# A fused convolution and linear-attention kernel: the first x group loaded and transposed in two pairs, another order of the first loads, six warm-up matmuls for nine, and a new written-out schedule

## The chip, the core and the metric

The kernel runs on one NeuronCore of a Trainium2 chip. The core has five instruction queues that run side by side and meet only at semaphores: PE (TensorE, matmuls and transposes into PSUM), DVE (VectorE), ACT (ScalarE), POOL (GpSimd) and SP (SyncE, which here issues every DMA). The metric is the device time of one execution in microseconds (us), lower is better; a time is the median of several runs.

## The reference

Two independent heads over a sequence of 2048 rows and 576 channels, put side by side in the output:

```python
def _A_ref(q, k, v, shift_k, ssm_k, ssm_D):
    k_pad = jnp.pad(k, ((0, 0), (ks - 1, 0), (0, 0)))
    for t in range(ks):                                   # ks = 4
        k_shift = k_shift + k_pad[:, t:t + S, :] * shift_k[:, ks - 1 - t]
    kv = k_shift * v
    y = irfft(rfft(kv, 2 * S) * rfft(ssm_k, 2 * S))[:S]   # long causal convolution
    y = y + kv * ssm_D
    return q * y

def _B_ref(x, wqkv, wo):                                  # 32 heads of 18 channels
    q, k, v = split(x @ wqkv)
    phi = lambda t: jnp.where(t > 0, t + 1, jnp.exp(t)) + 1e-6
    pq, pk = phi(q), phi(k)
    kv = jnp.einsum("bhsd,bhse->bhde", pk, v)
    z = jnp.einsum("bhsd->bhd", pk)
    num = jnp.einsum("bhqd,bhde->bhqe", pq, kv)
    den = jnp.einsum("bhqd,bhd->bhq", pq, z)[..., None] + 1e-6
    return (num / den) @ wo
```

All inputs are bf16.

## The kernel before

Both heads are written as one list of about 830 operations (`P.op`), each with the buffers it reads and writes. No scheduler runs: the text `PLAN` names the operations in the order in which they are issued, each with a letter for its engine (P for PE, A for ACT, D for DVE, G for POOL, S for SP), and `PLACES` gives the address of every buffer, PSUM banks included. Each engine therefore works through its own list strictly in the order written; an operation that may run on either of two engines ("AD", "DG") runs on the one whose letter the plan has. A buffer that reuses an address waits for the last user of it.

Head B. x is taken in four groups of 512 rows. `xt_load(g)` loads group g into `x_sb` (rows 4p to 4p+3 on partition p) and makes its transpose `xT`, which the projections need. For groups 1 to 3 (`XD`) a transposing DMA makes `xT`. For group 0, PE makes it: 16 transposes of 128x128 from `x_sb0` (L330) and four from `x40` (L328), where `x40` is a copy of channels 512 to 575 beside a block of ones; each of three PSUM tiles is then copied to `xT0` on DVE or ACT (L230 or L228). `kproj(r)` multiplies 128 rows by the key weights `wk` (ten matmuls, L606), ACT takes the exponential (`ek`, L611), and DVE makes the key feature in `pk` (L614). `qproj` does the same for queries (L627, L630, L633). `b_G(t)` (L656) contracts all of `x_sb` with all of `pk`: its first matmul needs the last of the 16 key features. After it come the small products (kv, z, den, M, msf), the normalisation of the queries through DRAM (`rden`, `rb`, `pqn`), and the output projection `b_out` (L796), whose rows leave through `ob`.

Head A is a Fourier transform in two matmul steps. The filter is transposed on PE (L419, copied to `hT`), step one is `s1` (L450, copied to `Ch` or `Cu` by ACT or DVE), then a 32x32 transpose on DVE (L489, `ct`), then step two (L498, copied to `sph` or `spu`). The key convolution is done on DVE in six pieces: two tap products (L389), two additions and the product with v (L235; some of these on POOL). Spectra are multiplied (`p1`, `p2`, L235), transformed back by `inv` (L534, copied to `V`) and `inv2` (L559), multiplied by q and stored.

The kernel starts with nine matmuls on a constant tile (`fill`, L827), whose result nobody reads; they need only a DVE memset of `cft` (L823). The first loads on SP are, in this order: x group 0, the constant tile `idw` (the identity and two small matrices), the shift weights `srow`, the tail of `wk` (channels 512 to 575, 72 KB) and then its main part (channels 0 to 511, 576 KB), two pieces of the filter (`hs`), the tail of `wq`, `Drow`, the main part of `wq`, the tables `Gsb`.

Of the kernel before, what the change touches and what calls it, by code (L numbers as in the profile page):

```python
# [9 lines left out]
BF = mybir.dt.bfloat16  # L10
# [4 lines left out]
D = 576  # L15
# [167 lines left out]
def kernel(  # L183
# [39 lines left out]
    def load(name, b, fn, nb, row, wr=None, rd=(), after=(), engs="S"):  # L223
        return P.op(engs, fn, rd=rd, wr=[b] if wr is None else wr, name=name, after=after, nb=nb, row=row)
# [79 lines left out]

    def xt_load(g):
        load("x", x_sb[g], lambda e: dma(e, x_sb[g].t[:].rearrange("p a d -> p (a d)"),
# [13 lines left out]
        for t0, tn in ((0, 2), (2, 2), (4, 1)):  # L320
            ps = psb(1, "xps")

            def tr(e, t0=t0, tn=tn, ps=ps):
                o = ps.t.rearrange("p b c -> p (b c)").bitcast(BF)
                for j in range(tn):
                    for i in range(4):
                        if t0 == 4:
                            nc.tensor.transpose(out=o[:, 128 * i:128 * i + 128], in_=x4[g].t[:, i, :], identity=ident())  # L328
                        else:
                            nc.tensor.transpose(out=o[:, 512 * j + 128 * i:512 * j + 128 * i + 128],  # L330
                                                in_=x_sb[g].t[:, i, 128 * (t0 + j):128 * (t0 + j) + 128], identity=ident())

            def ev(e, t0=t0, tn=tn, ps=ps):
                o = ps.t.rearrange("p b c -> p (b c)").bitcast(BF)
                copy(e, b.t[0:KT[t0], t0:t0 + tn, :].rearrange("p t n -> p (t n)"), o[0:KT[t0], 0:512 * tn])
            P.op("P", tr, rd=[(x4[g], "m"), (x4[g], "o"), idw] if t0 == 4 else [(x_sb[g], "m"), idw], wr=[ps], name="xtr", mm=[(128, 128, 128)] * (4 * tn), st="xtr%d" % g)
            P.op("DA", ev, rd=[ps], wr=[(b, t0)], name="xev", n=512 * tn, x2=1, st="xtr%d" % g)
# [259 lines left out]
    def kproj(r):  # L597
# [12 lines left out]
        P.op("P", mm, rd=[xT, wk], wr=[ps], name="k", mm=[(288, 128, 128)] * 10, st=st)  # L610
# [214 lines left out]
    def fmm(e):  # L825
        for j in range(9):
            nc.tensor.matmul(fps.t[:, 0, :], lhsT=cft.t[:, 0:128], rhs=cft.t[:], start=True, stop=True)  # L827
    P.op("P", fmm, rd=[cft], wr=[fps], name="fill", mm=[(512, 128, 128)] * 9)
# [24 lines left out]
G3 G4 S26 G6 G10 G5 G12 G1 D832 G14 G53 G8 S16 S18 P833 A27 P28 D29 P30 S50 P32 D31 S49 S361 S367 G2 A33 S52 P100  # L853
G9 G0 S21 P94 P97 P362 D23 A101 P368 A15 D102 A95 G224 D363 A98 S51 S19 G7 D99 A369 S20 D366 P91 A92 G11 P371 S419
A370 D96 A372 D93 G374 P364 A373 S474 P142 D365 A143 P376 D377 G375 P384 A385 P378 D379 D144 P145 A146 P386 D147
P382 D387 P380 S55 P148 G13 S37 P422 A383 A381 S36 P388 A149 D423 S24 P390 P420 P477 S468 A389 S47 D150 P439 G38
D421 P437 A391 A478 G424 P435 D440 P427 D436 S56 S42 A438 G48 S25 P433 D410 A428 S54 D392 P425 A426 P475 P431 A434
D476 P429 A430 P157 P471 P417 A432 P413 P399 D401 A472 A400 P395 P397 A398 S41 A414 A396 P469 D441 P166 D470 P444
S46 A158 S57 P408 P163 P393 P448 S39 D450 D409 A418 D159 P406 A167 A164 A407 D168 P151 A449 S44 A152 P442 A445 D165
P446 S226 P402 G43 G473 A443 G479 A447 D459 P139 P460 P160 A403 D153 A394 D71 S34 P415 P451 D70 A161 A140 P457 D162  # L860
A461 A416 D141 A452 P169 A458 P178 P453 P466 A454 P462 A463 P455 D72 P464 A456 D60 A465 P193 A467 P187 A170 P411
P404 S17 D61 A405 A412 A179 P109 P196 A194 A188 D180 P175 S225 D189 A197 G73 D171 S670 P184 S570 D195 A110 S669
D111 S628 A40 A185 G45 A176 D62 P112 P127 A113 D114 P172 D177 D186 P121 D198 P103 A128 G74 D129 A173 A122 D63 P181
D174 D123 P115 G35 P190 A104 G64 A182 D183 D105 A116 S569 D117 D81 P490 P130 A491 D80 A131 P492 P124 S549 A493 A125
P154 D132 P133 P118 S58 D126 S228 A155 A191 A134 A119 D82 P136 A137 D135 D156 S227 D120 D138 P106 A107 P482 P488
A483 D192 D108 G83 D84 P480 A481 P494 P219 D66 D65 A495 S59 S649 D75 A489 P486 S648 A220 P484 A487 P222 D76 P199
A223 A221 P232 D234 D233 D77 D78 A485 P204 A205 A206 P235 G79 A200 D236 D237 P239 D240 P207 P604 D238 A208 D241
P612 A613 S627 A201 S243 P214 D67 D68 A605 P614 P616 S242 D215 P602 S548 S256 D69 P217 D86 D85 D87 A615 A603 D88
D89 A617 P606 P610 P608 S255 A216 S244 A218 A611 P212 P533 S267 A609 P525 A607 A526 P535 A534 A536 S250 P209 G268
A210 A211 S254 P523 A524 P531 P202 S246 D245 A532 D514 P527 D496 P683 A213 A203 A528 G251 P695 A696 P229 D660 A684  # L870
P693 S252 D231 A694 P687 D230 P685 G247 A686 P277 P269 D688 D278 P689 A270 P273 P275 A274 P271 A276 D690 P515 P661
A272 A662 P681 A682 S263 G264 P691 S261 D253 S248 P279 D505 S259 G249 P503 A516 D692 P663 P497 P501 P667 A504 P508
A664 D280 A502 D509 P529 P298 D498 P311 P537 G262 P303 D639 G260 D299 A530 P306 A668 A538 D618 D539 A312 A307 P288
P665 A304 S257 P625 S22 P646 A289 P619 P621 A622 G258 P506 D620 A507 A626 P499 S265 P313 D581 S590 P308 A314 P286
D647 D560 A666 A309 A287 S90 S315 P283 S591 A284 P296 A297 S300 P623 P584 P510 G266 D500 S290 P586 S707 P540 P640
P321 A624 A541 D587 P323 A585 P318 D511 G671 A641 A322 P561 A319 A562 P563 A564 P519 P565 D739 P546 P642 P333 D566
A324 A547 D643 P336 A520 P326 P281 A334 A327 A282 P517 D337 D672 P512 A513 S727 P644 P544 P521 S706 P542 D518 A522
A545 A543 A645 P746 D697 P328 P353 P356 A357 D747 P346 P702 P567 A329 D354 A703 P704 P588 D718 S325 A589 A347 P700
P740 A741 P316 P293 A294 A701 A568 S749 A317 S285 S330 P291 P348 P358 A292 P338 A359 A705 S728 A349 S310 S320 A339
P673 G630 D629 P633 D650 P351 D651 P582 P744 D550 A674 P721 P742 D551 A634 P725 P331 A745 A583 P675 P301 S748 A743  # L880
P637 D726 S350 A676 A332 A302 P677 P719 A638 D572 P698 A352 P723 P679 P554 A678 A699 D750 P658 S360 D571 A724 P652
A720 P631 D592 D555 P656 A722 P552 A632 P556 P635 D593 P654 D751 A659 P558 A653 D553 A557 A657 P598 D636 A655 A680
S335 P600 P596 A597 A601 S340 A599 D709 P594 P573 P758 P798 A799 P784 D574 D708 A595 P575 S295 P579 P756 A785 P792
D576 D757 P577 A580 P796 S305 A559 P790 A578 P786 D730 D729 A787 P802 A791 D788 S355 A803 A797 P712 P768 P714 P710
A713 P762 D793 P774 A715 A769 A711 P766 D763 P780 G800 A775 S789 A759 P804 P760 D767 D770 S801 P731 S771 A805 P735
A736 D794 D761 D781 S795 P772 D764 A773 P778 S765 P737 D806 D776 P754 D755 A732 A779 P716 P752 P733 A717 A738 A753
P341 D782 P343 D734 D342 S807 A344 S777 S783 S345 P810 P808 D809 P826 P828 A811 P816 A829 D812 S813 P822 A823 D827
A817 P820 D830 S831 D821 D824 S825 D818 P814 D815 S819
"""
PLACES = """  # L890
# [47 lines left out]
```

## Time and profile before

| | us |
|---|---|
| median of 3 runs | 161.12 (161.06 to 161.38) |
| the profiled execution | 161.13 |
| its span, first to last instruction | 159.3 |
| around the span | 1.83 |

The profile is of one execution. Its page gives busy time by engine; the windows give the same for any stretch of time; the timeline lists the instructions in order; the chain of waits is followed back from the last instruction, and names at each step what released it. Matmuls overlap, and the page models their ends, so that PE counts as busy while it works through a queue slowly: a high PE share alone doesn't say that PE sets the pace. Where the records of two neighbouring instructions of one engine overlap by some hundredths of a microsecond, the distance of their starts is what they cost.

### The profile page before, as it was taken

What the parts mean: (1) busy time and instruction counts of PE and PEld (TensorE: products, weight loads), DVE (VectorE), ACT (ScalarE), POOL (GpSimd) and SP (SyncE); (2) the same over time, 40 slices, a digit from 0 to 9 for tenths busy, and PEclk for the clock granted to TensorE, in tenths of its full rate; (3) what the DMA queues carried; (4) which work ended last, traced back from release to release, by engine and by line L of the source; (5) the groups of instructions that cost most, each with busy time, mean ns of one, the idle gap of its engine ahead of it and who ended that gap; (6) DMA issues with size and microseconds to landing.
All of it is one profiled execution on the core that took longest, in us unless ns stands there. A gap on an engine that the chain in (4) does not pass through costs nothing.

```text
span 159.3 us, 4148 instructions
## 1 busy us (share of the span) xinstructions
PE 150.7 (95%) x1663; PEld 119.0 (75%) x1663; DVE 142.9 (90%) x173; ACT 126.5 (79%) x235; POOL 54.7 (34%) x48
## 2 busy tenths in 40 slices
PE   6899999999999999999999998999999999999980
PEld 2588888544568888788788887676677979999970
DVE  1318989999989999999999999999999999998981
ACT  3247899999997577784169799898999999889960
POOL 8802311200065940700340049899929000004000
PEclk9999999999999999999999999999999999999997
DMA  5999988999999204998014336864987735001875
GB/s 178 304 372 383 140 159 257 351 149 258 406 341 399 81 4 134 368 264 296 10 50 150 112 117 218 261 207 123 375 285 285 260 111 191 0 4 49 220 211 154
DMA packets 25629, 32.80 MB, mean 206 GB/s; under 512 B 15754, under 2 KB 20875, under 8 KB 24842
## 3 DMA queue, kind: packets, MB, share of 16 engines
q1 hardware_dynamic: 25610, 32.54, 67.8%
q8 instruction: 13, 0.21, 0.5%
q14 instruction: 6, 0.05, 0.1%
HBM read 20.86 MB, written 4.99 MB: 162 GB/s over the span
## 4 chain that ended last, share of the span: by engine, by line
PE 60%; DVE 26%; ACT 5%; DMA 3%; issue 2%; SPq 1%; DVEq 0%
PE ps_all L656 12%; PE ps_all L796 11%; PE ps_all L534 10%; PE ps_all L450 8%; DVE pqT L633 6%; DVE ct L489 5%; PE ps_all L559 5%; DVE pk L614 5%; DVE m L389 4%; PE ps_all L627 3%; PE ps_all L498 3%; PE ps_all L606 3%; DMA wk<-in_B_wqkv_dram 3%; DVE m L235 2%; PE ps_all L419 2%
## 5 line engine op out<-in xcount | busy, mean ns | idle before, releaser
L627 PE MATMUL ps_all<-xT,wq 128*126 128x512 bf16 (+1 forms) x100 | 24.5, 382 | 0.0
L796 PE MATMUL ps_all<-M,pqT 126*128 126x288 bf16 (+1 forms) x160 | 21.9, 287 | 0.3 <-ACT spu L228 0.3
L606 PE MATMUL ps_all<-wk,xT 128*128 128x288 bf16 x160 | 21.1, 286 | 0.6 <-DMA wk<-in_B_wqkv_dram 0.6
L389 DVE TENSOR_TENSOR m<-kh,Wj 128x3072 bf16<-128x3072 bf16 x12 | 20.5, 1754 | 0.0
L796 PEld LDWEIGHTS <-pqT 126*128 126x128 bf16 (+1 forms) x160 | 16.8, 110 | 4.6 <-issue 2.7
L606 PEld LDWEIGHTS <-xT 128*128 128x128 bf16 x160 | 17.4, 110 | 3.6 <-issue 1.0
L450 PEld LDWEIGHTS <-Gsb 128*128 128x128 bf16 x192 | 16.2, 98 | 4.0 <-issue 2.2
L228 ACT ACTIVATE Cu<-ps_all 128x768 bf16<-128x768 f32 x21 | 16.6, 862 | 1.7 <-PE ps_all L450 1.0
L627 PEld LDWEIGHTS <-wq 128*126 128x126 bf16 (+1 forms) x100 | 12.3, 131 | 7.3 <-issue 1.5
L534 PE MATMUL ps_all<-Esb,sph 128*128 128x128 bf16 x144 | 17.2, 219 | 0.0
L534 PE MATMUL ps_all<-Esb,X 128*128 128x128 bf16 x144 | 17.1, 219 | 0.0
L656 PE MATMUL ps_all<-pk,x_sb 128*128 128x289 bf16 (+1 forms) x128 | 17.1, 287 | 0.0
L235 POOL TENSOR_TENSOR pqT<-pqT,rb 126x1024 bf16<-126x1024 bf16 (+1 forms) x8 | 16.8, 2132 | 0.8 <-DVE pqT L235 0.6
L611 ACT ACTIVATE ek<-ps_all,neg 128x576 bf16<-128x576 f32 x16 | 11.9, 742 | 6.5 <-PE ps_all L606 5.6
L228 ACT ACTIVATE spu<-ps_all 128x512 bf16<-128x512 f32 x29 | 16.2, 620 | 0.7 <-DVE ct L489 0.7
L228 ACT ACTIVATE V<-ps_all 128x512 bf16<-128x512 f32 x28 | 15.8, 635 | 0.8 <-PE ps_all L534 0.4
L228 ACT ACTIVATE Ch<-ps_all 128x768 bf16<-128x768 f32 x19 | 15.3, 862 | 1.4 <-POOL v L235 1.0
L228 ACT ACTIVATE sph<-ps_all 128x512 bf16<-128x512 f32 x30 | 16.1, 628 | 0.4 <-PE ps_all L498 0.3
L630 ACT ACTIVATE eq<-ps_all,neg 126x512 bf16<-126x512 f32 (+1 forms) x20 | 13.2, 701 | 1.8 <-PE ps_all L627 1.8
L656 PEld LDWEIGHTS <-x_sb 128*128 128x128 bf16 x128 | 12.3, 98 | 3.2 <-issue 0.2
L235 DVE TENSOR_TENSOR m<-m 128x3072 bf16<-128x3072 bf16 (+1 forms) x10 | 14.4, 1442 | 0.1
L534 PEld LDWEIGHTS <-sph 128*128 128x128 bf16 x144 | 14.1, 98 | 0.4 <-issue 0.4
(94 smaller groups left out, 294.3 us busy)
## 6 DMA issues: line engine op xcount, KB each, us to landing
X<-sph SPq DMA_DIRECT2D x18, 256.0 KB
x_sb<-in_B_x_dram SPq DMA_DIRECT2D x4, 576.0 KB
v<-in_A_v_dram SPq DMA_DIRECT2D x2, 1152.0 KB
q<-in_A_q_dram SPq DMA_DIRECT2D x1, 2304.0 KB
out_dram<-ob SPq DMA_DIRECT2D x16, 144.0 KB
out_dram<-q SPq DMA_DIRECT2D x12, 192.0 KB
rb<-r_scr SPq DMA_DIRECT2D x8, 252.0 KB
kh<-in_A_k_dram SPq DMA_DIRECT2D x1, 1584.0 KB
```

The source lines that it names most:

```text
L228: nc.scalar.activation(out=o, in_=i, func=ACTF.Copy)
L235: return (nc.vector if e == "DVE" else nc.gpsimd).tensor_tensor(out=o, in0=a, in1=b, op=op)
L389: return nc.vector.tensor_tensor(out=m.t[:, i:i + 2], in0=i0, in1=i1, op=ALU.mult)
L450: nc.tensor.matmul(ps.t[:, bank, lo - 384 * bank:hi - 384 * bank], lhsT=Gsb.t[:, b, ri, :], rhs=src[:, lo - CC * j:hi - CC * j], start=Tru ...
L534: nc.tensor.matmul(ps.t[:, 0, 128 * c:128 * c + 128], lhsT=src.t[:, 4 * hh + c, :], rhs=Esb.t[:, 32 + wi, :], start=(wi == 0), stop=(wi == 1))
L606: nc.tensor.matmul(ps.t[:, hh, 0:HALF], lhsT=cols(xT.t[0:KT[t], t, :], r), rhs=wk.t[0:KT[t], t, HALF * hh:HALF * hh + HALF], start=(t == 0 ...
L611: P.op("A", lambda e: nc.scalar.activation(out=eb.t[:], in_=ps.t[:, :, 0:HALF], func=ACTF.Exp, bias=neg1.t[:]), rd=[ps, neg1], wr=[eb], na ...
L627: nc.tensor.matmul(ps.t[0:hn, 0, :], lhsT=wq.t[0:KT[t], t, h0:h0 + hn], rhs=xT.t[0:KT[t], t, :], start=(t == 0), stop=(t == 4))
L630: P.op("A", lambda e: nc.scalar.activation(out=eb.t[0:hn], in_=ps.t[0:hn, 0, :], func=ACTF.Exp, bias=neg1.t[0:hn, :]), rd=[ps, neg1], wr=[eb],
L633: P.op("D", lambda e: nc.vector.scalar_tensor_tensor(out=pqT[g // 2].t[0:hn, c, 512 * (g % 2):512 * (g % 2) + 512], in0=eb.t[0:hn], scalar ...
L656: nc.tensor.matmul(ps.t[0:m, 0, 0:n], lhsT=x4[r // 4].t[:, r % 4, :] if t == 4 else x_sb[r // 4].t[:, r % 4, 128 * t:128 * t + 128], rhs=p ...
L796: nc.tensor.matmul(ps.t[:, 0, 0:HALF], lhsT=cols(pqT[r // 8].t[0:kn, c, 512 * (r // 4 % 2):512 * (r // 4 % 2) + 512], r), rhs=M.t[0:kn, c, ...
```

## The change

- Group 0 goes through a new function, `x_pairs`. Its load is two DMAs of two rows per partition each, its copy to `x40` is two copies, and its transposes fill four PSUM tiles: for each pair one of eight transposes (channels 0 to 511) and one of two (from `x40`), each with its own copy to `xT0`.
- `kproj` of group 0 waits only for the pair that holds its rows, not for all of `xT0`.
- Six matmuls on the constant tile in place of nine.
- `PLAN` and `PLACES` are new throughout. Operations keep what they compute, but order, engines and addresses differ. (Operation numbers are four higher than before from about operation 35 on, since x_pairs adds four.)

The first loads on SP become: the second pair of x, `idw`, the first pair, the main part and then the tail of `wk`, two `hs`, half of `Gsb`, `Drow`, a third `hs`, the other half of `Gsb`, `srow`, then `wq` around a fourth `hs`. On DVE, `x_pairs` gives two copies to `x40` and four to `xT0`, one after the other (first pair's large copy, its small one, the second pair's small one, its large one). On PE the order behind the transposes is: key products of rows 0, 2 and 1, four filter tiles, and then steps one of the filter's transform; the fourth key product and all query products of group 0 come behind these, where before they stood ahead of them or between them.

```diff
+    def x_pairs(g):
+        b = SB("xT%d" % g, [128, 5, 512])
+        xTg.append(b)
+        for p in range(2):
+            load("xp", x_sb[g], lambda e, p=p: dma(e, x_sb[g].t[:, 2 * p:2 * p + 2].rearrange("p a d -> p (a d)"),
+                                                   ap(x, 512 * g * D + 2 * p * D, [[4 * D, 128], [1, 2 * D]])),
+                 294912, 2304, wr=[(x_sb[g], p)], engs=EARLY)
+            P.op("GDA", lambda e, p=p: copy(e, x4[g].t[:, 2 * p:2 * p + 2, 64:128], x_sb[g].t[:, 2 * p:2 * p + 2, 512:576]),
+                 rd=[(x_sb[g], p), (x4[g], "o")], wr=[(x4[g], ("m", p))], name="x4c", n=128, st="xtr%d" % g)
+        for p in range(2):
+            for t0, tn in ((0, 4), (4, 1)):
+                ps = psb(1, "xps")
+
+                def tr(e, t0=t0, tn=tn, ps=ps, p=p):
+                    o = ps.t.rearrange("p b c -> p (b c)").bitcast(BF)
+                    for j in range(tn):
+                        for i in range(2):
+                            nc.tensor.transpose(out=o[:, 256 * j + 128 * i:256 * j + 128 * i + 128],
+                                                in_=x4[g].t[:, 2 * p + i, :] if t0 == 4 else x_sb[g].t[:, 2 * p + i, 128 * j:128 * j + 128],
+                                                identity=ident())
+
+                def ev(e, t0=t0, tn=tn, ps=ps, p=p):
+                    o = ps.t.rearrange("p b c -> p (b c)").bitcast(BF)
+                    copy(e, b.t[:, t0:t0 + tn, 256 * p:256 * p + 256], o[:, 0:256 * tn].rearrange("p (t n) -> p t n", t=tn))
+                P.op("P", tr, rd=[(x4[g], ("m", p)), (x4[g], "o"), idw] if t0 == 4 else [(x_sb[g], p), idw], wr=[ps], name="xtr",
+                     mm=[(128, 128, 128)] * (2 * tn), st="xtr%d" % g)
+                P.op("DA", ev, rd=[ps], wr=[(b, (p, t0))], name="xev", n=256 * tn, x2=1, st="xtr%d" % g)
+
     def xt_load(g):
+        if g not in XD:
+            return x_pairs(g)
...
-        for t0, tn in ((0, 2), (2, 2), (4, 1)):
-            ps = psb(1, "xps")
...
-            P.op("P", tr, rd=[(x4[g], "m"), (x4[g], "o"), idw] if t0 == 4 else [(x_sb[g], "m"), idw], wr=[ps], name="xtr", mm=[(128, 128, 128)] * (4 * tn), st="xtr%d" % g)
-            P.op("DA", ev, rd=[ps], wr=[(b, t0)], name="xev", n=512 * tn, x2=1, st="xtr%d" % g)
...
-        P.op("P", mm, rd=[xT, wk], wr=[ps], name="k", mm=[(288, 128, 128)] * 10, st=st)
+        P.op("P", mm, rd=[wk] + ([xT] if r // 4 in XD else [(xT, (r % 4 // 2, t0)) for t0 in (0, 4)]), wr=[ps], name="k", mm=[(288, 128, 128)] * 10, st=st)
...
     def fmm(e):
-        for j in range(9):
+        for j in range(6):
...
-    P.op("P", fmm, rd=[cft], wr=[fps], name="fill", mm=[(512, 128, 128)] * 9)
+    P.op("P", fmm, rd=[cft], wr=[fps], name="fill", mm=[(512, 128, 128)] * 6)
...
 PLAN = """
-G3 G4 S26 G6 G10 G5 G12 G1 D832 G14 G53 G8 S16 S18 P833 A27 P28 D29 P30 S50 P32 D31 S49 S361 S367 G2 A33 S52 P100
...
+D836 G0 G57 G13 S28 G7 G11 G6 P837 S16 G5 S26 G1 A15 S53 S54 G9 P34 P30 G2 D29 G3 D27 P36 G14 D31 P32 D33 G8 P95
...
```

More of the change, by code (lines that the diff above doesn't have):

```diff
@@ L319, in xt_load @@
             return
-        for t0, tn in ((0, 2), (2, 2), (4, 1)):
-            ps = psb(1, "xps")
[L323 to L335, printed above, removed]
-            P.op("P", tr, rd=[(x4[g], "m"), (x4[g], "o"), idw] if t0 == 4 else [(x_sb[g], "m"), idw], wr=[ps], name="xtr", mm=[(128, 128, 128)] * (4 * tn), st="xtr%d" % g)
-            P.op("DA", ev, rd=[ps], wr=[(b, t0)], name="xev", n=512 * tn, x2=1, st="xtr%d" % g)
     def wload(which, key):
@@ L858 @@
[L858 to L872, printed above, removed]
@@ new lines @@
+P167 A114 A201 A192 D75 A168 G47 D199 G67 D115 P185 G483 D160 P122 A123 D193 P173 A174 D166 A49 D169 D76 A186 P107
+A108 G68 P179 D124 D187 S43 D202 D175 P137 D109 A180 A138 P134 S231 D77 D181 S38 G44 P119 S229 D139 G78 A135 D136
+P176 A120 S230 A177 P490 D121 P188 P494 A491 D178 A189 S652 A39 P496 A497 P110 P182 A495 A111 D84 D85 P488 A489
+S553 A183 D112 D86 S17 S62 P125 P140 A126 P128 S632 A141 D127 D87 D142 G88 D190 P131 A129 D130 A132 D184 P116 D133
+A117 P484 A485 S631 P194 S594 P535 P498 D118 P492 A493 A499 A195 S653 P223 D70 A224 P226 D69 P486 A487 A227 D196
@@ L889 @@
+P577 D584 P562 A578 P824 D825 S823 P285 S829 D286 S289 A563 P770 P772 A773 P766 A767 D771 D774 P764 P776 P778 A765
+D768 S775 S769 A779 A777 D780 P784 S781 P782 A785 A783 D786 S787
 """
 PLACES = """
[16 rows of a table removed]
[16 rows of a table added]
 """
```

48 lines of the change are left out of this document (28 added, 20 removed), and 32 rows, old and new, of the table PLACES.

## The prediction

> **What bounds the kernel now.** I read the page first, then the windows, the chain of waits and the timeline. By busy time PE is in front:
>
> ```profile
> PE 150.7 (95%) x1663; PEld 119.0 (75%) x1663; DVE 142.9 (90%) x173; ACT 126.5 (79%) x235; POOL 54.7 (34%) x48
> ```
>
> The reader is to see that two engines are nearly full, and that neither is named by its share alone, since stretched matmuls count as busy. The windows, cut where the first key feature starts on DVE, where DVE begins its transposes, where the last key feature ends, and where the last matmul ends, tell more (columns: window; its length, then busy us and count of PE, PEld, DVE, ACT, POOL; clock; DMA share; GB/s):
>
> ```profile
> 0.00:10.24 10.24, 8.13 (x48) 5.09 (x49) 1.95 (x5) 3.07 (x5) 6.55 (x20) 1.00 0.80 268
> 10.24:24.56 14.32, 14.31 (x150) 12.15 (x149) 11.89 (x18) 11.94 (x19) 2.47 (x5) 1.00 1.14 238
> 24.56:67.59 43.03, 42.64 (x357) 29.51 (x355) 42.62 (x49) 36.99 (x63) 15.48 (x10) 1.00 0.81 253
> 67.59:154.42 86.83, 85.29 (x1113) 72.19 (x1113) 84.88 (x101) 73.94 (x150) 30.23 (x13) 1.00 0.54 172
> 154.42:159.30 4.88, 0.32 (x4) 0.09 (x2) 1.56 (x4) 0.56 (x2) 0.00 (x0) 0.77 0.62 163
> ```
>
> DVE idles 8.29 us before the first key feature, 2.43 in the second window, 0.41 in the third: from 10.24 to 67.59 it is what the kernel waits for. The chain agrees, and shows where the lead passes to PE:
>
> ```profile
> 2.90 5.03 DMA wk<-in_B_wqkv_dram
> 7.98 3.84 PE ps_all L606 x30
> 11.81 0.99 PE ps_all L419 x16
> ...
> 66.41 0.61 DVE pqT L633
> 67.02 0.04 issue
> 67.06 0.94 PE ps_all L450 x8
> 68.00 1.98 PE ps_all L656 x16
> 69.98 0.66 PE ps_all L450 x8
> ...
> 109.20 0.60 ACT spu L228
> ...
> 154.42 0.02 issue
> 154.44 0.82 DVE q L235 x2
> ```
>
> The key weights land at 7.93 and start the projections. At 68.00 comes the first matmul that needs all sixteen key features; from there to 154.42 PE goes through its queue with 1.54 us of visible idle time (86.83 less 85.29), between 96 and 110 us mostly, where the chain runs over DVE and ACT copies. The last products and stores make 4.85 us of tail. So the time is made of five pieces: the lead-in up to the first key feature, DVE's work from there to the last one, its idle time among it, PE's queue from the first such matmul on, and the tail.
>
> **The lead-in.** Both inputs of the first projection are ready together before, within 0.05 us:
>
> ```profile
> 0.74 0.40 SPq L221 DMA_DIRECT2D x_sb<-in_B_x_dram  x1
> 1.21 0.41 SPq L221 DMA_DIRECT2D idw<-tab_i  x1
> 1.66 0.57 SPq L221 DMA_DIRECT2D srow<-in_A_shift_k_dram  x1
> 2.27 1.22 SPq L221 DMA_DIRECT2D wk<-in_B_wqkv_dram  x2
> 1.46 4.02 PE L827 MATMUL ps_all<-cft 128*128 128x512 bf16 x9 [1.46 <-DVE cft L823]
> 4.16 0.42 ACT L228 ACTIVATE x<-x_sb 128x256 bf16<-128x256 bf16 x1 [2.13 <-DMA x_sb<-in_B_x_dram]
> 5.28 1.83 PE L330 MATMUL ps_all<-idw,x_sb 128*128 128x128 bf16 x16
> 6.38 1.46 DVE L230 COPY xT<-ps_all 128x1024 bf16<-128x1024 bf16 x2 [4.97 <-PE ps_all L330]
> 7.37 0.60 ACT L228 ACTIVATE xT<-ps_all 128x512 bf16<-128x512 bf16 x1 [2.79 <-PE ps_all L328]
> 10.24 0.76 DVE L614 SCALAR_TENSOR_TENSOR pk<-ek,ps_all 128x576 bf16<-128x576 bf16 x1 [2.32 <-ACT ek L611]
> 24.56 2.36 DVE L489 STREAM_TRANSPOSE ct<-Ch 128x1024 f32<-128x1024 f32 x2
> ```
>
> x had landed at 4.16, but the fill held PE until 5.28: nine matmuls in 3.82, 0.425 each. Three fewer let the transposes begin at 4.00. The second pair is loaded first, and the first pair stands behind `idw`, so its data come some 0.3 late, near 4.5; its transposes are PE's second eight (0.106 each, a quarter of the fill's 0.425 for a quarter of its columns; eight of them from 5.28 and the copy at 6.38 leave 0.25 for the handover), from 4.86, so that it isn't waited for. They end at 5.7, the large copy runs from 5.95 to 6.64. The small copy (256 elements, not in the trace) lies between the 36-element row of 165 ns and the 768-element row of 520 ns quoted below; I take 200, near the 184 of the slope between the 768 and 1024 rows, so pair one is ready at 6.9 although DVE now does all six pieces (two x40 copies of 128 elements, 0.17 to 0.2 each by the same rows, lie in its idle time).
>
> The weights: their main part was issued from 2.86, as the fifth load. Now it is the fourth, without `srow` and the tail ahead, but the tail behind it: it is issued from 2.1, 0.75 earlier. The bytes ahead of the last weight row are the same but for `srow`'s, so the gain lies between 0 (bytes decide) and 0.75 (the issue decides). Between 4.00 and 5.50 the DMA engines moved 147 GB/s, between 5.50 and 7.50 394 GB/s:
>
> ```profile
> 4.00:5.50 1.50, 1.50 (x7) 0.67 (x6) 0.00 (x0) 0.42 (x1) 1.50 (x3) 1.00 0.77 147
> 5.50:7.50 2.00, 1.83 (x20) 1.72 (x19) 1.05 (x2) 0.13 (x1) 1.75 (x6) 1.00 1.06 394
> ```
>
> Bytes did not decide there, so I take 0.65: weights at 7.3, projections at 7.3, the first key feature at 9.6. **Lead-in: -0.65** (bounds 0 and -1.0, the latter if x alone decides).
>
> The saved fill has a price if it delays PE's full clock. The fill ran at 0.425 us for 512 columns; the thirty projections after 7.98 take 0.128 each for 288 columns, which is 0.227 for 512. The profile's clock column says 1.00 in both, so only the pace shows it: the rate doubled between 5.3 and 8.0, after a fill and twenty transposes. I let the transposes count as activity, and so charge nothing; the other case is a rival. The Trainium skill, "TensorE: Matmul & The Clock Gate", Part 4, says that transposes do not count as PE activity for the gate, and Part 1 that the gate opens after some 3.4 us of it; by that 2.55 us of fill would not do, the first projections would run at half pace until about 10.7, and the time would be some 1.7 us more. The fill of 3.82 us would satisfy either reading, so this trace can't decide it.
>
> **DVE up to the last key feature.** Counting its list in both plans between the first and the last key feature: one query feature (677 ns) goes behind, two `sph` copies (676) and one 1536-element addition (997, on POOL before) come in, and two 768-element filter copies become three of 512 (0.35 each by the slope of the next two rows).
>
> ```profile
> L633 DVE SCALAR_TENSOR_TENSOR pqT<-eq,ps_all 126x512 bf16<-126x512 bf16 x16 | 10.5, 677 | 0.5 <-ACT eq L630 0.4
> L230 DVE CAST V<-ps_all 128x512 bf16<-128x512 f32 x8 | 5.3, 688 | 0.0
> L235 DVE TENSOR_TENSOR m<-m 128x1536 bf16<-128x1536 bf16 x4 | 4.0, 997 | 0.1
> L230 DVE CAST sph<-ps_all 128x512 bf16<-128x512 f32 x6 | 4.0, 676 | 0.0
> L230 DVE CAST Cu<-ps_all 128x768 bf16<-128x768 f32 x3 | 2.8, 930 | 0.0
> L230 DVE COPY hT<-ps_all 128x1024 bf16<-128x1024 bf16 x4 | 2.8, 688 | 1.6 <-PE ps_all L419 1.6
> L230 DVE CAST ob<-ps_all 128x288 bf16<-128x288 f32 x4 | 1.8, 443 | 0.0
> L230 DVE COPY hT<-ps_all 128x768 bf16<-128x768 bf16 x2 | 1.0, 520 | 0.0
> L230 DVE COPY srt<-srow 64x36 bf16<-64x36 bf16 x1 | 0.2, 165 | 0.0
> L611 ACT ACTIVATE ek<-ps_all,neg 128x576 bf16<-128x576 f32 x16 | 11.9, 742 | 6.5 <-PE ps_all L606 5.6
> ```
>
> -0.68 + 1.35 + 1.00 + 0.01 and -0.17 for `srt`, which goes to ACT: **moved work +1.5**.
>
> **DVE's idle time in it** was 2.84 (2.43 + 0.41). The new list has key features 0 and 2, two filter copies, key feature 1, three filter copies, then copies of `Ch`. From PE's paces (1.28 a key product, a third of 3.84; 0.5 a filter tile, half of 0.99; 0.33 a step-one tile, half of 0.66) and 0.74 for an exponential I find it waiting 0.5 before the second feature, 0.4 before the first filter copy, 0.4 before the first `Ch` copy: 1.3, and 0.4 for the later stretch as before: 1.7. Bounds: 0.4, and 4.3 if it waits 1.5 us more than before. **-1.1**. The loads that this stretch needs have time: through the first half of `Gsb` 2.9 MB must land, at the first 10 us' 268 GB/s by 10.8, and step one begins near 13.2 (three key products and four filter tiles after 7.3).
>
> The last key feature then ends at 67.59 - 0.65 + 1.5 - 1.1 = 67.3: nearly where it did.
>
> **PE from there.** By the two lists, one tile of `Ch` and one of `Cu` more stand ahead of that first matmul, 0.33 each (0.66 for x8 above): **-0.66**. They fill time in which PE waited for DVE.
>
> **PE's waits after it.** DVE has less to do behind the last key feature: three `V` and two `Cu` copies go to ACT (-2.06, -1.86), the addition went ahead (-1.0); two `ob` copies (+0.89) and a query feature (+0.68) come. The other exchanges are of single instructions of such sizes and nearly cancel. So some -3.3 of 85, which ACT takes with 73.94 busy of 86.83. PE's 1.54 of visible waits should shrink; I take **-0.9** (bounds -1.5, and +1.0 by as much again in the other direction, since PSUM places are new).
>
> **The tail.** Before, the last inverse tiles are multiplied straight from PSUM. Now the last eight belong to another group, copied by ACT first (seven of eight), so that one copy and one 768-element product follow the last matmul, 1.0 to 1.4 us against 1.56 of DVE before, but PE must wait for the last `V` copies just ahead of these eight tiles. **+0.3** (bounds -0.3 and +0.9).
>
> Sum: 161.13 - 0.65 + 1.5 - 1.1 - 0.66 - 0.9 + 0.3 = **159.6**; the profiled execution stands 0.01 above the median.
>
> **Rivals.** A, the head start is eaten by the moved work: DVE's early list waits as long as before (2.84), and the late waits stay, since all key features come later. Place: DVE's queue between 9.6 and 68 us; 161.13 - 0.65 + 1.5 - 0.66 + 0.3 = 161.6, and 162.0 with 0.4 us of new waits. It decides once the last key feature ends after 68.0 (67.59 + 0.66 - 0.3). For it: DVE had only 0.41 idle in 43 us, so that added work lengthens that stretch one for one. Against it: idle time of 2.43 in front of it that the new order addresses. B, the clock opens later: by the removed 1.28 us, so between 6.6 and 9.3; at the late end 2.0 us of projections run at half pace, which loses 1.0: 160.6. For it: the doubling fell after the full fill. Against it: twenty transposes close behind the shorter one. The Trainium skill's rule on transposes, above, is this rival in a stronger form. C, the loads do not do what the order says: weights land at 7.93 as before, 160.2. D, the waits around 96 to 110 us vanish and DVE packs its early list without gaps: -0.6 and -1.0 more, 158.0; against it, chips have handovers that no list shows, 0.25 above.
>
> **Numbers.** Forecast 159.6, in 0.50 of cases (its own range 158.6 to 160.7); A 0.20, B 0.10, C 0.08, D 0.12. A measurement of this kernel tells 0.2% (0.32 us) from no change: faster means below 160.8, slower above 161.4. Faster: 0.47 + 0.02 + 0.06 + 0.06 + 0.12 = 0.73; slower 0.16 of A and 0.02 elsewhere, 0.18; the same, 0.09. Range 157.7 to 162.0: A and D are inside but for their far halves, some 0.15 left out.
>
> **What would show it.** Fill of 2.55 us; transposes from 4.0; first L606 at 7.3 (above 7.8: C); its pace 0.128 from the start (0.25: B); first L614 near 9.6; first L489 near 21 instead of 24.56; last L614 ending at 67.3 and first L656 right behind it (after 68.0: A); DVE idle between first and last L614 of 1.7; last L559 ending near 152.6, and 4.5 to 5.5 us of span behind it. Wrong altogether if DVE isn't what the first 67 us wait for, or if the tail after the last matmul passes 6 us.

## The result and the profile after

| | before | after |
|---|---|---|
| median, us | 161.09 (160.97 to 161.38, 4 runs) | 163.57 (162.84 to 164.27, 4 runs) |
| ratio after / before | | 1.0138 [1.0109, 1.0167] |
| the profiled execution | 161.13 | 163.53 |
| its span | 159.3 | 161.8 |

The changed kernel is 1.4% slower; 159.6 was forecast, with a range up to 162.0. Medians and extremes below are over all executions of a kernel; ratios leave out those that took over 1.5% more than the fastest of their kernel.

The windows of the changed kernel, cut at the same five events as before (first key feature on DVE, first 32x32 transpose on DVE, end of the last key feature, end of the last matmul; same columns):

```profile
0.00:11.49 11.49, 8.21 (x44) 5.09 (x45) 4.13 (x8) 2.23 (x3) 7.56 (x21) 1.00 0.81 271
11.49:25.57 14.08, 11.70 (x125) 10.56 (x123) 10.19 (x16) 8.43 (x12) 1.90 (x5) 0.88 1.13 275
25.57:71.69 46.12, 46.12 (x388) 32.46 (x386) 45.79 (x54) 40.40 (x68) 14.71 (x8) 1.00 0.77 218
71.69:156.34 84.65, 84.35 (x1106) 71.70 (x1104) 82.23 (x97) 72.48 (x148) 32.48 (x15) 1.00 0.53 175
156.34:161.80 5.46, 0.64 (x8) 0.41 (x6) 1.68 (x3) 1.64 (x5) 0.00 (x0) 0.88 0.65 179
```

Look at the first two rows and the clock in the second, 0.88. The first key feature starts 1.25 us later than before (11.49 against 10.24). From it to the last one DVE is busy for 10.19 + 45.79 = 55.98 us, 1.47 more than before, and idle for 60.20 - 55.98 = 4.22, where it was 2.84. From the last key feature to the last matmul the kernel is 2.18 faster (84.65 against 86.83), and the tail is 0.58 longer. The added DVE work was forecast. The lost time that was not, the late first key feature and DVE's new idle time (14.08 - 10.19 = 3.89 us in the second window, 2.43 before), lies in the first 26 us.

The timeline of the changed kernel there, PE, DVE and ACT (start, us, operation, and in brackets the idle time before it and what ended it):

```profile
1.46 2.74 PE L839 MATMUL ps_all<-cft 128*128 128x512 bf16 x6 [1.46 <-DVE cft L835]
4.00 1.06 PE L322 MATMUL ps_all<-idw,x_sb 128*128 128x128 bf16 x8
6.19 1.04 PE L322 MATMUL ps_all<-idw,x_sb 128*128 128x128 bf16 x8 [1.13 <-DMA x_sb<-in_B_x_dram]
8.34 0.88 PE L618 MATMUL ps_all<-wk,xT 128*128 128x288 bf16 x3 [0.69 <-DMA wk<-in_B_wqkv_dram]
...
15.52 1.08 DVE L230 COPY hT<-ps_all 128x512 bf16<-128x512 bf16 x3
16.70 0.60 ACT L228 ACTIVATE hT<-ps_all 128x512 bf16<-128x512 bf16 x1 [2.79 <-DVE hT L230]
17.34 2.71 PE L462 MATMUL ps_all<-hT,Gsb 128*128 128x192 bf16 x16 [2.23 <-ACT hT L228]
19.46 0.96 DVE L230 CAST Ch<-ps_all 128x768 bf16<-128x768 f32 x1 [2.85 <-PE ps_all L462]
```

Behind the constant matmuls PE has three holes in its first 18 us: 1.13 before the first pair's transposes, 0.69 before the projections, 2.23 before step one of the filter's transform. The last one is a chain of two engines. PE's filter tile is transposed into one PSUM tile; ACT copies half of its columns to `hT0`, DVE the other half to `hT1`. ACT's copy waits 2.79 us, until the last of DVE's three copies is done at 16.60, then PE waits for ACT, then DVE waits 2.85 for PE. Of the three only the last (operation 377) reads the tile that ACT reads; the two ahead of it in DVE's list read the tile before.

The chain of waits shows what these holes cost beside themselves:

```profile
2.14 6.16 DMA wk<-in_B_wqkv_dram
8.34 4.79 PE ps_all L618 x30
...
15.61 1.00 DVE hT L230 x3
17.34 2.71 PE ps_all L462 x16
```

The thirty projections take 4.79 us for the 3.84 of before, and the first 16 matmuls of step one 2.71, 0.17 each, where 0.08 each is the pace of before (0.66 for x8). Both run at half clock, the projections until 10.31 and step one throughout, as the windows of 3.41 us show, cut where the trace has its clock events (10.31 full, 17.14 half, 20.55 full):

```profile
3.48:6.90 3.42, 2.29 (x17) 1.61 (x16) 1.75 (x2) 0.00 (x0) 3.37 (x9) 1.00 0.94 271
6.90:10.31 3.41, 2.72 (x17) 1.81 (x15) 1.90 (x5) 0.00 (x0) 1.36 (x6) 1.00 0.98 372
10.31:13.72 3.41, 3.41 (x36) 2.89 (x35) 1.57 (x3) 2.04 (x3) 0.00 (x0) 1.00 1.05 409
13.72:17.14 3.42, 1.40 (x23) 1.28 (x22) 2.88 (x6) 0.63 (x2) 0.56 (x2) 1.00 1.03 231
17.14:20.55 3.41, 3.21 (x23) 3.01 (x23) 1.08 (x2) 2.15 (x4) 0.00 (x0) 0.50 1.27 157
20.55:23.96 3.41, 3.32 (x40) 2.88 (x39) 3.05 (x5) 2.77 (x5) 1.34 (x3) 1.00 1.14 374
```

The window that holds the 2.23 us wait has PE busy for 1.40 of 3.42, and the next one runs at 0.50. (The clock column says 1.00 before the first event of a trace; there the pace has to be read.) The Trainium skill, "TensorE: Matmul & The Clock Gate", Part 1, has windows of this length that run free of the kernel's start; the three events, 6.83 and 3.41 apart, agree with the length, and over the profiles the first event comes anywhere from 4.54 to 10.31.

### The profile page after: what moved, and what is told of

Read it like the earlier page. It is cut to its first block, busy times and chain, and to the rows that moved or that the text cites. A ratio compares the mean times of both kernels' runs of the same rounds, so it can differ in the third digit from the quotient of the medians.

```text
span 161.8 us, 4131 instructions
## 1 busy us (share of the span) xinstructions
PE 151.0 (93%) x1660; PEld 120.2 (74%) x1660; DVE 144.0 (89%) x175; ACT 125.2 (77%) x234; POOL 56.7 (35%) x49
## 4 chain that ended last, share of the span: by engine, by line
PE 71%; DVE 13%; ACT 6%; DMA 4%; issue 1%; POOL 1%; SPq 1%; ACTq 0%; POOLq 0%; DVEq 0%
PE ps_all L639 14%; PE ps_all L618 13%; PE ps_all L808 13%; PE ps_all L546 10%; PE ps_all L510 5%; PE ps_all L668 5%; PE ps_all L571 4%; PE ps_all L462 4%; DMA wk<-in_B_wqkv_dram 4%; ACT Cu L228 3%; DVE m L235 3%; DVE m L401 2%; DVE hT L230 2%; PE ps_all L431 2%; DVE rden L756 2%; DVE Ch L230 2%
## 5 line engine op out<-in xcount | busy, mean ns | idle before, releaser
L639 PE MATMUL ps_all<-xT,wq 128*126 128x512 bf16 (+1 forms) x100 | 24.0, 382 | 0.0
L618 PE MATMUL ps_all<-wk,xT 128*128 128x288 bf16 x160 | 21.9, 294 | 0.7 <-DMA wk<-in_B_wqkv_dram 0.7
L235 POOL TENSOR_TENSOR pqT<-pqT,rb 126x1024 bf16<-126x1024 bf16 (+1 forms) x9 | 18.9, 2128 | 9.1 <-ACT Cu L228 9.0
L228 ACT ACTIVATE Cu<-ps_all 128x768 bf16<-128x768 f32 x23 | 17.9, 852 | 4.2 <-PE ps_all L462 3.8
L462 PEld LDWEIGHTS <-Gsb 128*128 128x128 bf16 x192 | 17.0, 101 | 5.0 <-issue 2.9
L228 ACT ACTIVATE V<-ps_all 128x512 bf16<-128x512 f32 x31 | 18.6, 712 | 0.3 <-PE ps_all L546 0.2
L546 PE MATMUL ps_all<-Esb,sph 128*128 128x128 bf16 x144 | 17.8, 219 | 0.0
L546 PE MATMUL ps_all<-Esb,X 128*128 128x128 bf16 x144 | 17.8, 219 | 0.0
L228 ACT ACTIVATE spu<-ps_all 128x512 bf16<-128x512 f32 x27 | 15.1, 618 | 0.2 <-DVE ct L501 0.2
L626 DVE SCALAR_TENSOR_TENSOR pk<-ek,ps_all 128x576 bf16<-128x576 bf16 x16 | 11.7, 749 | 3.0 <-ACT ek L623 3.0
```

The lines of the kernel that those rows point to most:

```text
L228: nc.scalar.activation(out=o, in_=i, func=ACTF.Copy)
L235: return (nc.vector if e == "DVE" else nc.gpsimd).tensor_tensor(out=o, in0=a, in1=b, op=op)
L462: nc.tensor.matmul(ps.t[:, bank, lo - 384 * bank:hi - 384 * bank], lhsT=Gsb.t[:, b, ri, :], rhs=src[:, lo - CC * j:hi - CC * j], start=Tru ...
L546: nc.tensor.matmul(ps.t[:, 0, 128 * c:128 * c + 128], lhsT=src.t[:, 4 * hh + c, :], rhs=Esb.t[:, 32 + wi, :], start=(wi == 0), stop=(wi == 1))
L618: nc.tensor.matmul(ps.t[:, hh, 0:HALF], lhsT=cols(xT.t[0:KT[t], t, :], r), rhs=wk.t[0:KT[t], t, HALF * hh:HALF * hh + HALF], start=(t == 0 ...
L626: P.op("D", lambda e: nc.vector.scalar_tensor_tensor(out=pk[r // 4].t[:, r % 4, 0:D].rearrange("p (h c) -> p h c", h=2), in0=eb.t[:], scal ...
```

## The experiments

The theory after this reading, in three parts: (1) the order of the two copies on one PSUM tile makes PE wait for 1.5 us, (2) holes on PE shut the clock for a window, and (3) x in two halves lands late, so that six constant matmuls no longer reach to the next work. The rival is the prediction's case A: the VectorE work moved ahead of the last key feature sets the loss.

**One part undone at a time** (before on that chip: 160.88, 31 runs). Nine constant matmuls again:

```diff
-        for j in range(6):
+        for j in range(9):
```

> The changed kernel with nine constant matmuls instead of six, nothing else. Theory 'cold clock': the granted clock becomes full at about 6.9 us instead of 10.31, the thirty first key products run at 0.128 us each instead of 0.16 (4.79 us to about 3.85), the first key feature comes some 0.9 us earlier (11.49 to 10.6), and the time falls by 0.5 to 1.0 us from 163.57. Rival 'late data': the clock opens when the projections run, whatever stands before them; the first key products stay at 4.79 us and the time within 0.3 us.

Measured: 162.31, ratio 1.0072 [1.0038, 1.0106]. The projections start at 7.75 at full pace (30 in 3.84), but PE still waits 2.2 us before step one. Three executions lie at 160.9 to 161.1 with a mean clock of 0.995 or more, seven at 162.2 to 162.9 with 0.989 or less.

The first x group in one transfer, issued first, its transposes still in two pairs:

```diff
-            load("xp", ... x_sb[g].t[:, 2 * p:2 * p + 2] ... [[4 * D, 128], [1, 2 * D]]
+            load("xp", ... x_sb[g].t[:] ... [[4 * D, 128], [1, 4 * D]] ... if p else None
```

> The changed kernel with the first x group loaded whole in one DMA that stands first (the second pair's load does all, the first pair's does nothing); transposes, order and plan as changed. Theory 'late data': x lands near 4.1 us for both pairs (6.17 for the first pair now), PE's 1.1 us of waiting between its transposes goes, the data side is ready at about 6.9 and the first key product starts when the weights land, 7.4 to 8.3; time lower by 0.3 to 1.0 us. Rival: the weights land at 8.3 whatever x does, the first key product stays at 8.34, and the time within 0.3 us.

Measured: 162.06, ratio 1.0031 [0.9996, 1.0066]; again a group at 160.6 to 160.9 with a clock of 0.995 or more, and one from 161.9 up with 0.989 or less. In the profiled execution, one of the first group, PE waits as long before step one, and the clock stays up:

```profile
15.75 1.48 PE L462 MATMUL ps_all<-hT,Gsb 128*128 128x192 bf16 x16 [2.23 <-ACT hT L228]
```

The wait lies across two windows here:

```profile
11.42:14.84 3.42, 2.10 (x33) 1.98 (x32) 3.30 (x7) 0.74 (x1) 0.03 (x1) 1.00 1.05 298
14.84:18.25 3.41, 2.50 (x33) 2.47 (x33) 1.48 (x4) 2.57 (x4) 0.53 (x2) 1.00 1.41 236
```

ScalarE's copy ahead of VectorE's in the plan:

```diff
-... P375 D377 A376
+... P375 A376 D377
```

These two neighbours stand on different engines, so the exchange leaves the list of each engine as it was. Only which of the two waits for the other changes.

> The changed kernel with two neighbours of the plan exchanged: ScalarE's hT copy stands before VectorE's copy of the same PSUM tile. Theory 'copy queue': ScalarE's copy waited 2.8 us for VectorE's three hT copies; now it starts at about 15.1 instead of 16.70, step one of the filter (L462) starts near 15.8 instead of 17.34, the clock does not fall to half at 17.14 us, and the first L501 transpose comes 2 to 3 us earlier than 25.57; time lower by 1.0 to 2.5 us from 163.57. Rival: the copy waits for something else (PE's transposes or an address), step one still starts at 17.3, and the time within 0.3 us.

Measured: 161.38, ratio 0.9997 [0.9958, 1.0036]. The best executions, 159.48 twice, lie 1.4 us below the median of the kernel before and 0.9 below its fastest. In the profiled one, 161.96, PE waits 0.69 us before step one, but the clock was shut from 8.92 to 12.34, behind another hole, PE's wait for the key weights:

```profile
8.40 5.50 PE L618 MATMUL ps_all<-wk,xT 128*128 128x288 bf16 x30 [1.95 <-DMA wk<-in_B_wqkv_dram]
```

The same kernel once more, beside the runs of the third group below:

> The changed kernel with ScalarE's copy first and nothing else, once more, on the chip of the other three. If six constant matmuls leave TensorE idle often enough in the first 8 us for the clock to be shut in some executions, the times fall in two groups, 159.5 to 159.9 and 1.3 to 3 us above. If the order of the copies was the whole loss, all of them lie at 159.5 to 160.

Measured: 161.34, ratio 0.9981 [0.9942, 1.0020], from 159.63 to 162.55: four executions at 159.6 to 160.3 with a clock of 0.994 or more, five at 161.3 to 161.9 with 0.985 to 0.989, and the slowest at 1.00, which the clock doesn't explain. Two windows of its profile:

```profile
4.81:8.22 3.41, 1.03 (x15) 0.77 (x13) 1.93 (x5) 0.00 (x0) 3.30 (x9) 1.00 0.97 278
8.22:11.63 3.41, 3.12 (x14) 1.92 (x14) 0.04 (x1) 0.53 (x1) 0.10 (x2) 0.50 1.03 405
```

Here a window fell so that only 1.03 us of work lay in it, and the projections began at half clock. In four of the six profiles of the changed kernel with six constant matmuls PE is done 1.80 to 1.95 us before the projections can start, in one of them with x in one transfer, so halves of x aren't needed for it; in the six with nine it is 0.64 to 1.48. With such a hole it depends on where the window falls whether an execution belongs to the first group of times or to the second.

Six constant matmuls in the kernel before, to price that edit alone:

```diff
-        for j in range(9):
+        for j in range(6):
```

> The kernel before with six constant matmuls instead of nine, nothing else. Theory 'cold clock': the transposes end near 6.0 instead of 7.3, PE then idles until the weights land at 7.93, the clock becomes full at 10.3 instead of 6.88, the thirty first key products take 4.7 to 4.9 us instead of 3.84, and the time rises by 0.4 to 1.0 us from 161.1. Rival 'transposes and projections are activity enough': full clock at 6.9 or with the first key product, 3.84 us, and the time within 0.3 us of 161.1.

Measured: 160.75, ratio 1.0013 [0.9977, 1.0048]; seven of ten executions at 160.4 to 161.0, three at 162.3 to 162.5, two of these at a clock of 1.00, which the clock doesn't explain. With x landing at 4 us the three matmuls cost nothing in most executions, as the prediction had it.

**The parts together** (before on that chip: 160.97, 13 runs). The changed kernel itself as the yardstick:

> The changed kernel itself, beside the kernel before, as the yardstick for the three runs sent with it. Both theories expect 163 to 164 us, the profiled landing of the first x half at 6 us or a little below, and at least one stretch of half clock between 8 and 21 us.

Measured: 163.27, ratio 1.0141 [1.0080, 1.0203].

All three parts undone (nine matmuls, x in one transfer, ScalarE's copy first):

> The changed kernel with the nine constant matmuls back, the first x group in one transfer issued first, and ScalarE's copy ahead of VectorE's three on the shared PSUM tile. Theory 1 (gaps on TensorE in the first 18 us close the clock gate, and everything behind is late by it; the moved VectorE work is affordable): no half clock after 7 us, first s1 matmul near 14.6, first L501 near 22.3, last key feature end 68.5, span 157.5, time 159.0 to 159.8, so faster than before by about 1 %. Theory 2 (the VectorE work moved ahead of the last key feature sets the loss, wherever TensorE's gaps lie): last key feature end still 70 or later, time 161 to 162.

Measured: 159.51 (159.24 to 159.92), ratio 0.9919 [0.9889, 0.9949].

Nine matmuls and ScalarE's copy first, x in its two pairs:

> The changed kernel with nine constant matmuls and ScalarE's copy first, the first x group still in two pairs, identity second. If the two pairs matter only through the gap at 5 to 6 us, which nine constant matmuls fill, then no half clock and 159.2 to 160 us as in the run with all three parts. If the late landing of the pairs itself costs, the transposes of x start after 5.5 us, the gate still closes in some executions and the time is 160.5 to 162.

Measured: 159.64 (159.53 to 159.81), ratio 0.9919 [0.9899, 0.9939]. The two beat the kernel before by 1.3 to 1.5 us, with the whole rest of the change in them, and the slowest execution of either is 0.7 below the fastest of before beside them (160.61). The moved VectorE work, which both keep, can't be the loss: the rival falls. The windows of the second one, cut at the same five events:

```profile
0.00:10.36 10.36, 7.55 (x47) 4.50 (x48) 4.11 (x7) 2.23 (x3) 7.56 (x21) 1.00 0.79 261
10.36:21.55 11.19, 10.37 (x126) 9.37 (x124) 10.15 (x17) 8.36 (x12) 0.98 (x3) 1.00 1.16 256
21.55:67.66 46.11, 46.11 (x387) 32.47 (x386) 45.78 (x54) 40.38 (x68) 15.73 (x10) 1.00 0.86 249
67.66:152.31 84.65, 84.34 (x1106) 71.68 (x1104) 82.24 (x97) 72.51 (x148) 32.50 (x15) 1.00 0.54 174
152.31:157.70 5.39, 0.64 (x8) 0.41 (x5) 1.68 (x3) 1.64 (x5) 0.00 (x0) 0.84 0.68 185
```

The last three rows are those of the changed kernel to within 0.1 us; the second is 14.08 - 11.19 = 2.89 shorter and the first 1.13. That is all but 0.1 of the difference of 4.1 in span. Its timeline shows what became of the wait:

```profile
14.02 0.60 ACT L228 ACTIVATE hT<-ps_all 128x512 bf16<-128x512 bf16 x1 [1.24 <-PE ps_all L431]
14.40 1.08 DVE L230 COPY hT<-ps_all 128x512 bf16<-128x512 bf16 x3
14.67 1.48 PE L462 MATMUL ps_all<-hT,Gsb 128*128 128x192 bf16 x16 [0.69 <-ACT hT L228]
...
15.86 0.99 DVE L230 CAST Ch<-ps_all 128x768 bf16<-128x768 f32 x1 [0.38 <-PE ps_all L462]
```

ACT copies as soon as PE has transposed, PE waits 0.69 in place of 2.23, 16 matmuls take 1.48 in place of 2.71, and DVE waits 0.38 in place of 2.85. ACT's copy and DVE's first one, of the tile before, overlap by 0.22 us here. Both write `hT0`, so the buffer written doesn't keep the engines apart; what is left is the shared PSUM tile. From the start of the projections to that of step one it is 6.50 us (8.17 to 14.67) against 9.00 (8.34 to 17.34): 0.95 of the 2.50 is the half clock in the projections, 1.55 the wait. From there to the first 32x32 transpose it is 6.88 against 8.23: 1.35, which is the half clock behind the wait. With 0.17 in the start, these sum to 4.02.

One transfer and ScalarE's copy first, six matmuls kept:

> The changed kernel with the first x group in one transfer and ScalarE's copy first, six constant matmuls kept. If the three constant matmuls left out cost nothing by themselves once x lands early (the prediction charged nothing for them), the same time as with all three parts, 159.0 to 159.8. If six are too few to open the clock, k matmuls start at half clock (30 of them in 4.8 us or more in place of 3.84) and the time is 160.5 to 161.5.

Measured: 159.58, ratio 0.9939 [0.9906, 0.9972]: six executions at 159.0 to 159.6, and four at 160.7 to 161.1, three of these with a clock of 0.986 or 0.987. With nine matmuls and ScalarE's copy first, in none of the 28 executions of the four kernels that have both (two of them further below) is the mean clock under 0.992; six don't always keep it there.

**The order of the copies alone, and the moved work** (before on that chip: 161.22, 31 runs). Nine matmuls and x in one transfer, but VectorE's copies first:

> The changed kernel with nine constant matmuls and the first x group in one transfer, but with VectorE's three copies ahead of ScalarE's one on the shared PSUM tile, as the change has them. If that order by itself makes TensorE wait near 15 us: first s1 matmul 1.4 to 1.6 us later than in the run with all three parts (near 15.7), time at least 160.7, and 162.2 in the executions in which the clock falls to half behind the wait. If the two other parts were what mattered, 159.2 to 159.8.

Measured: 161.60 (160.75 to 162.81), ratio 1.0014 [0.9977, 1.0051]; five executions at 160.7 to 161.3 with a clock of 0.996 or more, five at 161.9 to 162.8 with 0.985 to 0.989. Against the kernel with all three parts (on another chip) the first s1 matmul is 1.5 us later (15.72 against 14.22). Windows of its profile:

```profile
12.81:16.22 3.41, 1.18 (x18) 1.06 (x17) 2.17 (x5) 0.60 (x1) 0.56 (x2) 1.00 1.06 237
16.22:19.63 3.41, 3.41 (x29) 3.34 (x28) 1.75 (x3) 2.52 (x4) 0.00 (x0) 0.50 1.23 195
```

Its first group (median 160.86) is 0.36 below the kernel before, the kernel with all three parts 1.46, each beside its own runs of before: the order costs 1.1 by the wait, and in half of the executions, where the wait takes up most of one clock window, 1.4 more (median of the second group 162.25). Profiles of single executions give the two prices apart. With x in one transfer, six matmuls and VectorE's copies first (160.63 us, shown above) the wait is there and the clock stays up: the first 32x32 transpose is at 22.62 and the last key feature starts at 68.0. With nothing but the copies exchanged (159.53 us, the last run of the group before, on another chip) these are 21.04 and 66.4: 1.6 us for the wait alone, of which 1.3 is left in the span (158.9 against 157.6). In the profile just shown they are 23.90 and 69.3: 1.3 more, in the span too (160.2), for the half clock behind the same wait of 2.23.

The 1536-element addition (operation 87) back on GpSimd, in the kernel with nine matmuls and ScalarE's copy first:

```diff
-... S17 S62 ... D87 ...
+... S17 S62 ... G87 ...
```

> The changed kernel with nine constant matmuls and ScalarE's copy first, and with the 1536-element addition of the filter (the prediction's +1.00 of moved work) on GpSimd, where the kernel before has it. By the prediction's sum VectorE sets the end of the last key feature: it ends some 0.9 us earlier, near 66.7, and the time is 158.7 to 159.2. If TensorE's own queue up to there is the limit by now, the key feature moves less than 0.3 and the time stays at 159.5 to 159.8.

Measured: 160.97 (160.56 to 161.26), ratio 0.9980 [0.9959, 1.0001]: worse than with the addition on VectorE, which neither expectation had. The same with x in one transfer:

> The same with the first x group in one transfer. If the halves of x landing by 5.2 are early enough behind nine constant matmuls, the same time as with the pairs, within 0.3 us; if the half microsecond by which the key weights land earlier comes through, 0.3 to 0.5 less than with the pairs.

Measured: 160.72, ratio 0.9976 [0.9947, 1.0004], so 0.25 apart, within their intervals; the pairs aren't worth their second transfer, but cost little once the fill covers them. In the first of the two, from the first key feature to the end of the last it is 57.18 us against 57.30 without the edit: 0.95 taken from DVE came back as 0.1. That fits PE, which is busy there without a gap (46.11 of 46.11 in the third window above); no run takes work from PE there. What was lost stands in the instructions on the filter tile `m` between 66 and 73 us (fastest, median and slowest in ns; first and last start), of this kernel:

```profile
L401 DVE TENSOR_TENSOR m<-kh,Wj x2: 1745/2302/2860, 67.2 to 70.0; 128x3072 bf16<-128x3072 bf16 x2
L235 POOL TENSOR_TENSOR v<-m,v x1: 3094/3094/3094, 65.3 to 65.3; 128x1536 bf16<-128x1536 bf16 x1
```

and of the one without the edit:

```profile
L401 DVE TENSOR_TENSOR m<-kh,Wj x2: 1751/1752/1752, 67.6 to 69.2; 128x3072 bf16<-128x3072 bf16 x2
L235 POOL TENSOR_TENSOR v<-m,v x1: 3099/3099/3099, 63.9 to 63.9; 128x1536 bf16<-128x1536 bf16 x1
```

GpSimd's product now runs until 68.4, past the start of VectorE's at 67.2, and that one takes 2.86 us in place of 1.75. The other kernel with the edit has the same (2.85). The 1.1 lost there is about what the kernel lost as a whole; that the one made the other is read from the sizes, not tested.

## Why the prediction failed

Its five pieces, in us, against the time before (161.13), as measured in the profile of the changed kernel and in that with nine matmuls and ScalarE's copy first:

| step | predicted | changed kernel | the two parts undone |
|---|---|---|---|
| lead-in to the first key feature | -0.65 | +1.25 | +0.12 |
| VectorE work up to the last one | +1.5 | +1.47 | +1.42 |
| VectorE idle among it | -1.1 | +1.38 | -1.47 |
| last key feature to last matmul | -0.66 - 0.9 = -1.56 | -2.18 | -2.18 |
| tail | +0.3 | +0.58 | +0.51 |
| sum | 159.6 | 163.6 (profiled 163.53) | 159.5 (profiled 159.65) |

**The step that failed** is "DVE's idle time in it ... 1.7", measured 4.22, and in it one wait, "0.4 before the first `Ch` copy", measured 2.85. (The wait before the second feature was 0.54 for 0.5, the one before the first filter copy 0.12 for 0.4.) The step took the waits from the paces of PE and ACT, as if the two copies of one PSUM tile ran side by side. They don't, and the order in the plan decides who waits: 1.55 us before step one, and 1.35 of half clock behind the wait. With the two exchanged that wait is 0.38, and DVE idles for 11.19 + 46.11 - 55.93 = 1.37, less than the 1.7 forecast. The term's own upper bound, 4.3, covers the 4.22; the lead-in's bounds, 0 and -1.0, don't cover its +1.25. The trace shows that ACT waits for DVE on a tile that both only read. The Trainium skill, "PSUM — Partial Sum Buffer", section "PSUM bank collisions raise a hardware error", says that two engines must be kept apart on the same partitions of one bank, reads against reads too. The runs agree in that the second reader is held behind the first in either order: with ACT first, DVE's copy of the tile starts at 15.07, after ACT's end at 14.62, and waits for ACT's semaphore. No run here shows what would happen without the wait.

**The lead-in** failed in its loads and in the clock. The first pair's "data come some 0.3 late, near 4.5": 15 of 16 DMA engines had delivered the first pair by 5.15 and the last at 6.14 in this profile, and all of it by 5.05 in the other profile of the same kernel. The weights, forecast at 7.3, landed at 8.30, where they had come at 7.93: rival C, and worse. Over the runs they landed between 7.71 and 8.46 with x in pairs (seven profiles) and between 7.62 and 7.67 with x in one transfer (five), which lies inside the 7.38 and 7.93 that the old order shows in two. So in these profiles the new order of the loads brought nothing, and with a second transfer of x the weights came 0.1 to 0.8 later. The two copies to `x40`, "0.17 to 0.2 each", took 1.01 and 0.95 (last section); the weights came later still, so this cost nothing. "I let the transposes count as activity, and so charge nothing" holds by itself, see below; but it left out that six matmuls and the eight transposes of the pair at hand are over by 5.06, so that PE idled until 6.19, the window had 2.29 of 3.42 us of work and the clock opened at 10.31. That is rival B at its place and at its price (0.95 lost, 1.0 forecast), though by idle time and not because transposes don't count. That the price agrees is luck: the clock opened a whole microsecond after B's latest time, 9.3, and the projections began a whole microsecond after 7.3. It is not in every execution: in the second profile of this kernel the projections ran at full pace.

**What held.** The transposes from 4.00; the moved work to 0.03 us; the stretch behind the last key feature, where the two terms together were 0.6 too small a gain; the tail inside its bounds. Rival A's sign came out, at its decisive point too (the last key feature after 68.0: it ended at 71.7), but not by its mechanism: the work was there in the kernels that run in 159.5 as well. And the reading that VectorE sets the pace up to the last key feature was half of the truth. There PE was busy 42.64 of 43.03 us before and shows no gap after, and 0.95 us taken from DVE gave 0.1.

## What to carry to other kernels

In a schedule written out by hand, two readers of one PSUM tile on different engines can be a dependence, as they were here, and the order in the text sets its direction: put first the one whose result the matmuls wait for. A wait on TensorE costs more than its length where it fills most of a clock window, so the start of a kernel is to be planned for TensorE's idle time in each 3.4 us, and warm-up matmuls are to be counted by when the data land. When only some executions are slow, sort them by mean clock before averaging. Here that doesn't sort all of them: 162.88 and 162.55 with ScalarE's copy first, 162.22 with x in one transfer and the addition on GpSimd, and two executions at 162.3 of the kernel before with six matmuls have a mean clock of 1.00, and what slowed them stays open.

## What the runs showed of the hardware

**When the clock falls and rises.** Over the first 30 us of the profiles, in windows of 3.41 us in the phase of each trace's own clock events: the clock fell after windows with PE busy for 1.03, 1.18 (twice), 1.32, 1.40 and 1.46 us, and stayed up after 1.58 and 1.61. The two nearest to the edge, and the window behind the first of them, from the run of ScalarE's copy first and from that of x in one transfer:

```profile
5.51:8.92 3.41, 1.46 (x17) 1.11 (x18) 2.28 (x5) 0.00 (x0) 2.70 (x8) 1.00 0.86 275
8.92:12.34 3.42, 3.42 (x17) 2.12 (x16) 0.76 (x1) 0.74 (x1) 0.00 (x0) 0.50 1.02 414
```

```profile
4.60:8.01 3.41, 1.58 (x23) 1.45 (x23) 1.89 (x6) 0.00 (x0) 3.30 (x9) 1.00 0.98 336
```

In the changed kernel's profile above it did not open after 2.29 and opened after 2.72. No idle window is needed to shut it; 0.43 of one was too little work.

**Transposes count.** In the run with x in one transfer, ScalarE's copy first and six matmuls, the first clock event (full) is at 7.03. The two windows ahead of it:

```profile
0.20:3.62 3.42, 2.16 (x6) 0.74 (x6) 0.48 (x1) 1.49 (x2) 2.98 (x9) 1.00 0.51 177
3.62:7.03 3.41, 2.88 (x22) 2.13 (x20) 1.15 (x3) 0.00 (x0) 3.35 (x9) 1.00 0.93 279
```

The second one holds two matmuls of the fill, 0.59 us, and twenty transposes, 2.29. Without the transposes it would be 0.17 busy, far below the 2.29 us that did not open the clock elsewhere; it opened it, and the projections ran at full pace from 7.68. The Trainium skill, "TensorE: Matmul & The Clock Gate", Part 4, says that transposes in PE's transpose mode do not count in the same way; these do. (The trace lists them as matmuls and doesn't tell whether they ran in that mode.)

**VectorE behind GpSimd.** A product of two SBUF tiles on VectorE that started inside one on GpSimd took 2.86 us in place of 1.75 (rows above). The Trainium skill, "SBUF — State Buffer", section "SBUF: two separate sides", calls the port that the two share an exclusive lock held for a whole instruction; the rows agree to 0.14 us (GpSimd ends at 68.43, VectorE 1.61 later). A copy can be held in the same way. These rows of the changed kernel are a memset on GpSimd and the second copy to `x40`:

```profile
6.11 0.95 POOL L279 MEMSET pqT<- 64x1024 bf16 x1
6.17 0.95 DVE L230 COPY x<-x_sb 128x128 bf16<-128x128 bf16 x1 [1.39 <-DMA x_sb<-in_B_x_dram]
```

In all twelve profiles of the changed kernel and its variants both copies to `x40` end 0.05 to 0.09 us after the end of a memset, wherever they started, and take 0.29 to 1.15 us.
